# Two banks more for the first batch's scores, an earlier split of x, and weight decodes spread evenly in a fused attention and two-MLP kernel

## The chip, the cores and the metric

The kernel runs on one core of a Trainium2 chip. A core has a matrix engine (TensorE, PE in the profile, with its weight loads as PEld), VectorE (DVE), ScalarE (ACT), GpSimd (POOL) and SyncE (SP), which here issues every DMA. TensorE writes its results into PSUM banks, and the other engines read them there; everything else lies in SBUF. Each engine works through its own list of instructions in order and waits on semaphores for the others. The metric is the device time of one execution in microseconds (us), lower is better.

## The reference

The input is a batch of 4 with 8 heads, 576 positions and head size 64, all in 32-bit floats. Shortened to its arithmetic:

```
scores = scale * q @ k.T, causal mask;  local = softmax(scores) @ v
q_p = elu(q) + 1;  mem_out = (q_p @ M_prev) / (q_p . z_prev + 1e-6)
x = sigmoid(beta) * mem_out + (1 - sigmoid(beta)) * local     # to [2304, 512]
x = (s * relu(x @ w_in)**2 + b) @ w_out                       # first MLP, 2048 wide
h = x @ w2_in;  z = h * softmax(h)
out = (layernorm(z) * g_ln) @ w2_out                          # second MLP, 1024 wide
```

Weights and activations of the MLPs are split into a high and a low part, so that each of their products is three matmuls (high by high, low activation by high weight, high activation by low weight).

## The kernel before, in words

**Attention.** The heads are taken in pairs: 4 batches of 4 pairs, 16 pairs in all (`NPAIR` is 4, `u` counts the pairs). A pair goes through five steps of scores. `scores(u, 0, 1)`, then chunk 2, chunk 3 and the tail (`CF` is 4) each write one PSUM tile `s`, which `ps_s` gives out: it has a single buffer of two banks (L193, L305), one bank for each head of the pair, or for each half of the tail. VectorE reads the tile, adds the mask and finds the row's extreme (L331, L349), ScalarE takes the exponential (L298), TensorE transposes the result (L372), ScalarE copies the transposes out (L375), and `values` multiplies them with v (L404, L407) and adds the memory part (L409, L410). GpSimd multiplies v by the gate (L236), makes the product `q` for the memory's denominator (L251), and scales rows (L269, L270, L355). Transposes and values follow the scores with a lag of two steps.

**The weights.** They come as bit patterns that `decode` (L141 to L168) rebuilds: a DMA (L147), then one operation on ScalarE (L152), four on VectorE (L153, L154, L156, L158), one on GpSimd (L159), one more on ScalarE (L163) and one on VectorE (L164). 48 decodes serve the whole kernel. `decode_to(n)` asks for the first n of them, and where it is called sets how early a decode stands in the program.

**The first MLP** has two parts. `first_part` (five of the sixteen columns of weights, `FP1`) works on half batches of 288 tokens and serves as filler between the attention's steps: `split_x` makes `xh` on ScalarE (L442) and `xl` on VectorE (L443), `hidden` makes `h` (L424 to L426) with a relu on ScalarE (L427), a square on VectorE (L434) and the split parts `g` (L435, L438); then `y` (L471 to L473) is copied out by ScalarE (L475) and stored. During the attention `h` and `y` share `ps_m`, two buffers of one bank. What is left of the filler when the attention ends runs in a loop at L567 with PSUM tiles of its own for `h` (`ps_h`, two buffers). `second_part` does the other eleven columns in ten rounds of up to 512 tokens; a round loads `xr` from `xd` (L493), splits it with the same two lines (L442, L443) and runs `hidden` and `ystep` (L608 to L610). In round 0 the split is told to stand behind the last copy of the first part, `lastact` (L588). The second MLP follows.

**Order.** The kernel is built with a scheduler that takes the instructions as the code lists them and places them on each engine by its own estimate of when their operands are ready. So a buffer that is free earlier, or a decode that is called later, moves instructions on every engine. `issue_after` holds an instruction behind another one.

Of the kernel before, what the change touches and what calls it, by code (L numbers as in the profile page):

```python
# [8 lines left out]
F32 = mybir.dt.float32  # L9
# [3 lines left out]
AF = mybir.ActivationFunctionType  # L13
# [4 lines left out]
P = 128  # L18
# [5 lines left out]
def attention_mlp_kernel(  # L24
# [9 lines left out]
    nc = tc.nc  # L34
    B, NPAIR, _, NCH, _, D = q.shape
# [18 lines left out]
    big = const.tile([P, (CF + 1) * P], F32, name="big")  # L54
# [4 lines left out]
    HS = S // 2  # L59
    mtail = const.tile([P, HS], F32, name="mtail")  # L60
# [5 lines left out]
    gate = const.tile([P, H], F32, name="gate")  # L66
# [33 lines left out]
    RA = 2 * FP1 + 8  # L100
    RB = 25 - RA
# [68 lines left out]
    decoded = [0]  # L170
# [13 lines left out]
    QT = S + CF * P  # L184
# [3 lines left out]
    class Attention:  # L188
# [111 lines left out]
        def scores(self, u, *cs):  # L300


            p = self.pair[u]
            raw = p["raw"]
            ss = self.ps_s.tile([P, 2, 512], F32, tag="s", name=f"s{u}_{cs[0]}")  # L305
            if cs[0] == CF:
                self.tail_scores(u, ss)
                return
            c0 = 0
            at = {}  # L310
            for i in cs:
                for k in range(i + 1):
                    for j in range(2):
                        x = raw[j * D:(j + 1) * D]
                        self.last = nc.tensor.matmul(ss[:, j, c0 + k * P:c0 + (k + 1) * P],  # L315
                                                     x[:, S + i * P:S + (i + 1) * P], x[:, k * P:(k + 1) * P],
                                                     start=True, stop=True).ins
                at[i] = c0
                c0 += (i + 1) * P
            if "sums" not in p:  # L320
                p["sums"] = self.tiny.tile([P, NCH, 2], F32, tag="sums", name=f"sums{u}", bufs=2)

                nc.gpsimd.memset(p["sums"][:, CF], 1.0)
            for i in cs:
                n = (i + 1) * P
                prs, mxs = [], []
                for j in range(2):
                    pr = p["pr", 2 * i + j] = self.sp.tile([P, n], F32, tag=f"pr{i}", name=f"pr{u}_{i}_{j}")

                    mx = self.tiny.tile([P, 1], F32, tag="mx", name="mx")  # L330
                    nc.vector.tensor_tensor_reduce(pr, ss[:, j, at[i]:at[i] + n],  # L331
                                                   big[:, CF * P - i * P:CF * P - i * P + n],
                                                   -scale, FMAX, ALU.add, ALU.min, mx)
                    prs.append(pr)
                    mxs.append(mx)
                self.exps(prs, mxs, [p["sums"][:, i, e:e + 1] for e in (0, 1)])

        def tail_scores(self, u, ss):

            p = self.pair[u]  # L340
            raw = p["raw"]
            pr = p["pr", 2 * CF] = self.sp.tile([P, S], F32, tag="prt", name=f"pr{u}_t", bufs=1)
            mx = None
            for t in range(2):
                cols = slice(t * HS, (t + 1) * HS)
                nc.tensor.matmul(ss[:, t, 0:HS], raw[:, QT:RL], raw[:, cols], start=True, stop=True)
                m0 = FMAX if t == 0 else mx
                mx = self.tiny.tile([P, 1], F32, tag="mx", name="mx")
                nc.vector.tensor_tensor_reduce(pr[:, cols], ss[:, t, 0:HS], (big[:, cols], mtail)[t], -scale, m0,  # L349
                                               ALU.add, ALU.min, mx)  # L350
# [64 lines left out]


    attended = [False]
    lastact = [None]

    def hidden(w, xh, xl, n, ps, r, gh, gl, square=False):  # L420

# [25 lines left out]
    def first_part(b, pools):  # L447

        xs, gs, ys, _ = pools
        for sub in range(2):  # L450
            nm = f"{b}_{sub}"
            x = xbs[b][:, :, sub * N1:(sub + 1) * N1]
            xh = xs.tile([P, NC, N1], F32R, tag="xh", name=f"xh{nm}")
            xl = xs.tile([P, NC, N1], F32R, tag="xl", name=f"xl{nm}")
            split_x(x, xh, xl)
            gq = []
            for f in range(FP1):
                ps = pools[3][0].tile([P, 512], F32, tag="mh"[len(pools[3]) - 1], name=f"h{nm}_{f}")
                r = gs.tile([P, N1], F32, tag="r", name=f"r{nm}_{f}", bufs=2)
                g = gs.tile([P, 2, N1], F32R, tag="g", name=f"g{nm}_{f}")  # L460
                decode_to(f + 1)
                hidden(wtiles["in", f], xh, xl, N1, ps[:, 0:N1], r, g[:, 0], g[:, 1])
                gq.append(g)
                yield
            for c in range(NC):
                ps = pools[3][-1].tile([P, 512], F32, tag="m", name=f"y{nm}_{c}")
                o = ps[:, 0:N1]
                decode_to(2 * FP1)
                for f in range(FP1):
                    wc = [wtiles["out", f][:, t, c * P:(c + 1) * P] for t in range(2)]  # L470
                    nc.tensor.matmul(o, wc[0], gq[f][:, 0], start=(f == 0), stop=False)  # L471
                    nc.tensor.matmul(o, wc[1], gq[f][:, 0], start=False, stop=False)
                    nc.tensor.matmul(o, wc[0], gq[f][:, 1], start=False, stop=(f == FP1 - 1))  # L473
                y = ys.tile([P, N1], F32, tag="y", name=f"yo{nm}_{c}")
                lastact[0] = nc.scalar.activation(y, o, AF.Copy).ins  # L475
                t0 = b * S + sub * N1
                nc.sync.dma_start(yd[:, c, t0:t0 + N1], y)
                yield
# [19 lines left out]
    with ExitStack() as fctx:  # L498
# [65 lines left out]
        fpools[3] = [ps_h, ps_m]  # L564
        load2(0, False)
        attended[0] = True
        for it in filler:  # L567
            for _ in it:
                decode_to(min(decoded[0] + 1, RA + RB))

    def second_part():
        load2(0, True)
# [4 lines left out]
        for ri, (fs, bi) in enumerate(rounds):  # L577
# [10 lines left out]
            with tc.issue_after(lastact[0]) if ri == 0 else nullcontext():  # L588
                split_x(x[:, :, 0:n], xh[:, :, 0:n], xl[:, :, 0:n])
# [22 lines left out]
            for i, f in enumerate(fs):  # L612
                hstep(f)
                if i >= 1:
                    ystep(fs[i - 1])
                step += 1
                if ri == 0:
                    decode_to(min(decoded[0] + 2, g2))
                elif ri < len(blocks):

                    decode_to(g2 + (late - g2) * step // steps)
                elif ri < last:

                    decode_to(late + (last2 - late) * step // steps)
                else:
                    decode_to(decoded[0] + 1)
                if ri == last and i == 2:

                    z = dec.tile([P, WN, 2], I32, tag="raw", name="z0").rearrange("p n t -> p (n t)").bitcast(F32)
                    first["z"] = weights_of(0, z, *(const.tile([P, 1], F32, name=f"t0_{k}") for k in range(3)))  # L630
            if ri == last:
                decode_to(NW)
                first[1] = products(1)
# [164 lines left out]
```

## Time and profile before

| | us |
|---|---|
| median of 3 runs (lowest and highest) | 884.39 (883.9 to 886.73) |
| the profiled execution, device time | 885.48 |
| its span, first to last instruction | 883.70 |
| busy: PE, DVE, ACT, POOL | 850.8, 539.9, 513.7, 182.8 |

The profiled execution is 1.09 us above the median, and 1.78 us of it lie outside the span. TensorE is busy for 96% of the span, so what it does not do is 32.9 us in all. A busy TensorE is not one at its peak, since the ends of matmuls are modelled. The granted clock of TensorE is the full one, 2.4 GHz, except for one short stretch behind 375 us, where it is the lower level, 1.2 GHz.

### The profile page before, as it was taken

The page shows a single profiled execution, that of the slowest core. Times are in us where ns is not written, and L with a number is a line of the kernel's source. Part 1 is how long each engine was busy: PE and PEld are TensorE (multiplying, and loading weights), DVE is VectorE, ACT ScalarE, POOL GpSimd, SP SyncE. Part 2 cuts the span into 40 slices and gives each one's busy share as a digit, 9 for nine tenths or more (in the row PEclk, how much of TensorE's full clock was granted, in tenths as well). Part 3 has the DMA queues.
Part 4 walks back from the last instruction along what each step waited for, and adds up shares of the span by engine and source line. Part 5 has one row for each costly group of instructions (what it writes and reads, how often), then busy time and mean ns, then how long its engine had stood idle before and what let it go on. Part 6 is the DMA issues. An engine that isn't in the chain of part 4 may idle for free.

```text
span 883.7 us, 14245 instructions
## 1 busy us (share of the span) xinstructions
PE 850.8 (96%) x5344; PEld 699.0 (79%) x5344; DVE 539.9 (61%) x1236; ACT 513.7 (58%) x1094; POOL 182.8 (21%) x180
## 2 busy tenths in 40 slices
PE   7899889999999999899999999999999999999997
PEld 5677668888878878878888888888988888888885
DVE  3898986768778467922338864454775444454532
ACT  4776765666666665555558776556774333433332
POOL 4445351332333222200002311101120000000000
PEclk9999999999999999999999999999999999999999
DMA  7445242533343204472013422111200000000000
GB/s 228 133 148 184 79 155 59 155 97 119 115 149 118 69 1 156 147 263 95 3 45 114 144 100 96 48 48 55 89 24 1 25 25 23 13 24 24 25 25 36
DMA packets 41494, 76.44 MB, mean 86 GB/s; under 512 B 6352, under 2 KB 20176, under 8 KB 41424
## 3 DMA queue, kind: packets, MB, share of 16 engines
q1 hardware_dynamic: 41424, 75.52, 26.5%
q8 instruction: 42, 0.69, 0.3%
q14 instruction: 28, 0.23, 0.1%
HBM read 61.35 MB, written 14.16 MB: 85 GB/s over the span
## 4 chain that ended last, share of the span: by engine, by line
PE 78%; DVE 13%; ACT 3%; issue 2%; POOL 1%; DMA 1%; POOLq 0%; SPq 0%; ACTq 0%; DVEq 0%
PE h L424 7%; PE h L425 7%; PE h L426 7%; PE y L609 5%; PE y L608 5%; PE y L610 5%; PE h L665 4%; PE h L666 4%; PE h L667 4%; PE o L730 4%; PE o L729 4%; PE o L728 4%; PE pp L372 3%; PE s L315 3%; PE po L404 3%
## 5 line engine op out<-in xcount | busy, mean ns | idle before, releaser
L425 PE MATMUL h<-xl,w 128*128 128x512 f32 (+2 forms) x380 | 131.0, 345 | 2.1 <-DVE xl L443 2.1
L159 POOL TENSOR_TENSOR wa<-wa,raw 128x512 f32<-128x512 f32 x48 | 67.8, 1415 | 314.5 <-DVE raw L158 198.2
L424 PE MATMUL h<-xh,w 128*128 128x512 f32 (+2 forms) x380 | 130.0, 349 | 2.8 <-ACT xh L442 2.5
L426 PE MATMUL h<-xh,w 128*128 128x512 f32 (+2 forms) x380 | 129.2, 341 | 0.0
L427 ACT ACTIVATE r<-h 128x512 f32<-128x512 f32 (+2 forms) x95 | 45.6, 489 | 87.3 <-PE h L426 73.0
L298 ACT ACTIVATE pr<-pr,mx 128x128 f32<-128x128 f32 (+3 forms) x128 | 70.8, 555 | 37.5 <-DVE mx L331 37.5
L432 DVE TENSOR_TENSOR gl<-r,gh 128x512 fp32r<-128x512 f32 (+1 forms) x55 | 37.2, 685 | 88.1 <-ACT r L431 88.0
L424 PEld LDWEIGHTS h<-xh,w 128*128 128x128 f32 x380 | 70.9, 188 | 15.2 <-ACT xh L442 3.5
L425 PEld LDWEIGHTS h<-xl,w 128*128 128x128 f32 x380 | 71.5, 188 | 13.1 <-DVE xl L443 3.8
L608 PE MATMUL y<-gh,w 128*128 128x512 f32 (+1 forms) x220 | 80.8, 372 | 0.0
L609 PE MATMUL y<-gh,w 128*128 128x512 f32 (+1 forms) x220 | 80.8, 372 | 0.0
L426 PEld LDWEIGHTS h<-xh,w 128*128 128x128 f32 x380 | 71.5, 188 | 8.1 <-issue 0.4
L331 DVE CUSTOM_DVE_ANT_0 pr<-s,big 128x128 f32<-128x128 f32 (+3 forms) x128 | 56.2, 485 | 9.6 <-PE s L315 9.2
L375 ACT ACTIVATE pt<-pp 128x256 f32<-128x256 f32 (+2 forms) x96 | 47.2, 518 | 22.5 <-PE pp L372 22.0
L610 PE MATMUL y<-gl,w 128*128 128x512 f32 (+1 forms) x220 | 60.0, 372 | 0.0
L728 PE MATMUL o<-w,zh 128*128 128x512 f32 x144 | 56.8, 395 | 0.8 <-ACT zh L722 0.8
L730 PE MATMUL o<-w,zl 128*128 128x512 f32 x144 | 56.9, 395 | 0.6 <-DVE zl L723 0.6
L667 PE MATMUL h<-w,yl 128*128 128x512 f32 x144 | 56.6, 393 | 0.0
L729 PE MATMUL o<-w,zh 128*128 128x512 f32 x144 | 56.6, 393 | 0.0
L665 PE MATMUL h<-w,yh 128*128 128x512 f32 x144 | 56.6, 393 | 0.0
L666 PE MATMUL h<-w,yh 128*128 128x512 f32 x144 | 56.6, 393 | 0.0
L315 PEld LDWEIGHTS s<-kq 64*128 64x128 f32 x640 | 40.1, 187 | 19.3 <-issue 6.7
(142 smaller groups left out, 1959.1 us busy)
## 6 DMA issues: line engine op xcount, KB each, us to landing
raw<-in_moe_w_in_dram SPq DMA_DIRECT2D x24, 512.0 KB, 3.8
raw<-in_moe_w_out_dram SPq DMA_DIRECT2D x24, 512.0 KB, 3.5
kq<-in_kq_dram SPq DMA_DIRECT2D x16, 608.0 KB, 4.0
xr<-xd SPq DMA_DIRECT2D x8, 1024.0 KB, 5.9
q<-in_q_dram SPq DMA_DIRECT2D x16, 320.0 KB, 3.0
v<-in_v_dram SPq DMA_DIRECT2D x16, 320.0 KB, 3.1
xd<-xb SPq DMA_DIRECT2D x4, 1152.0 KB, 6.5
yd<-yo SPq DMA_DIRECT2D x32, 144.0 KB, 2.4
```

What stands on the lines that cost most here:

```text
L424: nc.tensor.matmul(ps, wc[0], xh[:, c, 0:n], start=(c == 0), stop=False)
L425: nc.tensor.matmul(ps, wc[0], xl[:, c, 0:n], start=False, stop=False)
L426: nc.tensor.matmul(ps, wc[1], xh[:, c, 0:n], start=False, stop=(c == NC - 1))
L608: nc.tensor.matmul(o, wc[0], gh[:, 0:n], start=(f == fs[0]), stop=False)
L609: nc.tensor.matmul(o, wc[1], gh[:, 0:n], start=False, stop=False)
L610: nc.tensor.matmul(o, wc[0], gl[:, 0:n], start=False, stop=(f == fs[-1]))
L665: nc.tensor.matmul(o, yh[:, c], w[:, 0], start=(c == 0), stop=False)
L666: nc.tensor.matmul(o, yh[:, c], w[:, 1], start=False, stop=False)
L667: nc.tensor.matmul(o, yl[:, c], w[:, 0], start=False, stop=(c == NC - 1))
L728: nc.tensor.matmul(oo, zh, w[:, 0], start=(f == 0), stop=False)
L729: nc.tensor.matmul(oo, zh, w[:, 1], start=False, stop=False)
L730: nc.tensor.matmul(oo, zl, w[:, 0], start=False, stop=(f == NF2 - 1))
```

## The change

Four edits. The scores of chunk 2 and of the tail, for the four pairs of the first batch, take two tiles of one bank from `ps_m` in place of the one tile of `ps_s`; so in this batch consecutive score tiles alternate between the two pools. The split of `xr` in round 0 is no longer held behind the last copy of the first part. The decodes are called at other places: in the filler's rest one in every fourth step in place of every step (5 in place of 7), in round 0 one in every second step in place of none beyond those already done (3), and from there evenly to the same count as before at the end of round 4. Three one-column constants of the second MLP's start lie in columns of the old `gate` tile.

```
--- before.py
+++ after.py
@@ -302,7 +302,12 @@
 
             p = self.pair[u]
             raw = p["raw"]
-            ss = self.ps_s.tile([P, 2, 512], F32, tag="s", name=f"s{u}_{cs[0]}")
+            if u < NPAIR and cs[0] in (2, CF):
+
+                ss = [ps_m.tile([P, 512], F32, tag="m", name=f"s{u}_{cs[0]}_{j}") for j in range(2)]
+            else:
+                ss = self.ps_s.tile([P, 2, 512], F32, tag="s", name=f"s{u}_{cs[0]}")
+                ss = [ss[:, j] for j in range(2)]
             if cs[0] == CF:
                 self.tail_scores(u, ss)
                 return
@@ -312,7 +317,7 @@
                 for k in range(i + 1):
                     for j in range(2):
                         x = raw[j * D:(j + 1) * D]
-                        self.last = nc.tensor.matmul(ss[:, j, c0 + k * P:c0 + (k + 1) * P],
+                        self.last = nc.tensor.matmul(ss[j][:, c0 + k * P:c0 + (k + 1) * P],
                                                      x[:, S + i * P:S + (i + 1) * P], x[:, k * P:(k + 1) * P],
                                                      start=True, stop=True).ins
                 at[i] = c0
@@ -328,7 +333,7 @@
                     pr = p["pr", 2 * i + j] = self.sp.tile([P, n], F32, tag=f"pr{i}", name=f"pr{u}_{i}_{j}")
 
                     mx = self.tiny.tile([P, 1], F32, tag="mx", name="mx")
-                    nc.vector.tensor_tensor_reduce(pr, ss[:, j, at[i]:at[i] + n],
+                    nc.vector.tensor_tensor_reduce(pr, ss[j][:, at[i]:at[i] + n],
                                                    big[:, CF * P - i * P:CF * P - i * P + n],
                                                    -scale, FMAX, ALU.add, ALU.min, mx)
                     prs.append(pr)
@@ -343,10 +348,10 @@
             mx = None
             for t in range(2):
                 cols = slice(t * HS, (t + 1) * HS)
-                nc.tensor.matmul(ss[:, t, 0:HS], raw[:, QT:RL], raw[:, cols], start=True, stop=True)
+                nc.tensor.matmul(ss[t][:, 0:HS], raw[:, QT:RL], raw[:, cols], start=True, stop=True)
                 m0 = FMAX if t == 0 else mx
                 mx = self.tiny.tile([P, 1], F32, tag="mx", name="mx")
-                nc.vector.tensor_tensor_reduce(pr[:, cols], ss[:, t, 0:HS], (big[:, cols], mtail)[t], -scale, m0,
+                nc.vector.tensor_tensor_reduce(pr[:, cols], ss[t][:, 0:HS], (big[:, cols], mtail)[t], -scale, m0,
                                                ALU.add, ALU.min, mx)
             sm = self.tiny.tile([P, 1], F32, tag="sm", name="sm")
             self.exps([pr], [mx], [sm])
@@ -415,7 +420,6 @@
 
 
     attended = [False]
-    lastact = [None]
 
     def hidden(w, xh, xl, n, ps, r, gh, gl, square=False):
 
@@ -472,7 +476,7 @@
                     nc.tensor.matmul(o, wc[1], gq[f][:, 0], start=False, stop=False)
                     nc.tensor.matmul(o, wc[0], gq[f][:, 1], start=False, stop=(f == FP1 - 1))
                 y = ys.tile([P, N1], F32, tag="y", name=f"yo{nm}_{c}")
-                lastact[0] = nc.scalar.activation(y, o, AF.Copy).ins
+                nc.scalar.activation(y, o, AF.Copy)
                 t0 = b * S + sub * N1
                 nc.sync.dma_start(yd[:, c, t0:t0 + N1], y)
                 yield
@@ -564,9 +568,11 @@
         fpools[3] = [ps_h, ps_m]
         load2(0, False)
         attended[0] = True
+        turn = 0
         for it in filler:
             for _ in it:
-                decode_to(min(decoded[0] + 1, RA + RB))
+                turn += 1
+                decode_to(min(decoded[0] + (turn % 4 == 0), RA + RB))
 
     def second_part():
         load2(0, True)
@@ -585,8 +591,7 @@
             x = xq.pop(ri)
             xh = xs2.tile([P, NC, NB], F32R, tag="xh", name=f"xh2_{ri}")
             xl = xs2.tile([P, NC, NB], F32R, tag="xl", name=f"xl2_{ri}")
-            with tc.issue_after(lastact[0]) if ri == 0 else nullcontext():
-                split_x(x[:, :, 0:n], xh[:, :, 0:n], xl[:, :, 0:n])
+            split_x(x[:, :, 0:n], xh[:, :, 0:n], xl[:, :, 0:n])
             ys = [ps_y.tile([P, 512], F32, tag=f"y{c}", name=f"y2_{ri}_{c}") for c in range(NC)]
             gq = {}
 
@@ -615,10 +620,11 @@
                     ystep(fs[i - 1])
                 step += 1
                 if ri == 0:
-                    decode_to(min(decoded[0] + 2, g2))
+                    decode_to(decoded[0] + step % 2)
+                    early = decoded[0]
                 elif ri < len(blocks):
 
-                    decode_to(g2 + (late - g2) * step // steps)
+                    decode_to(early + (late - early) * step // steps)
                 elif ri < last:
 
                     decode_to(late + (last2 - late) * step // steps)
@@ -627,7 +633,7 @@
                 if ri == last and i == 2:
 
                     z = dec.tile([P, WN, 2], I32, tag="raw", name="z0").rearrange("p n t -> p (n t)").bitcast(F32)
-                    first["z"] = weights_of(0, z, *(const.tile([P, 1], F32, name=f"t0_{k}") for k in range(3)))
+                    first["z"] = weights_of(0, z, *(gate[:, k:k + 1] for k in range(3)))
             if ri == last:
                 decode_to(NW)
                 first[1] = products(1)
```

How the first edit moves TensorE's list, from pair 0's tail scores on (`s_4` is the tail, `s_0`, `s_2`, `s_3` are the other steps; pair 0 reads `kq_139`, pair 1 `kq_165`; `pp` are transposes, `po` is values, `tr`, `tp`, `tq` are transposes for the memory part). Before:

```order
L346 MATMUL s_4_291<-kq_139 128x288
L404 MATMUL po_399<-pt_1_312,v_173 64x256 x6
L404 MATMUL po_399<-pt_1_312,v_173 64x128 x2
L315 MATMUL s_0_335<-kq_165 128x128 x6
L279 MATMUL tr_372<-ident,r_308 128x128 x4
L289 MATMUL tp_380<-ident,ph_175 128x128 x4
L292 MATMUL tq_386<-ident,ph_175 128x128
L315 MATMUL s_2_429<-kq_165 128x128 x6
L372 MATMUL pp_8_389<-ident,pr_t 128x128 x4
```

And now:

```order
L351 MATMUL s_4_0_292<-kq_139 128x288
L320 MATMUL s_0_337<-kq_165 128x128 x6
L351 MATMUL s_4_1_293<-kq_139 128x288
L377 MATMUL pp_6_362<-ident,pr_3_0_267 128x128 x4
L409 MATMUL po_401<-pt_0_253,v_173 64x256 x2
L409 MATMUL po_401<-pt_0_253,v_173 64x128
L377 MATMUL pp_7_368<-ident,pr_3_1_270 128x128 x4
L409 MATMUL po_401<-pt_0_253,v_173 64x128
L320 MATMUL s_2_0_431<-kq_165 128x128 x3
L320 MATMUL s_2_1_432<-kq_165 128x128 x3
L279 MATMUL tr_374<-ident,r_310 128x128 x4
```

Pair 1's first scores stand between the halves of pair 0's tail, and its second scores in front of the memory transposes. The first hidden products of the first MLP, which stood between the pairs of this batch, now stand behind the last of its scores.

GpSimd's list at the same place (`v_173` and `v_186` are the v of pairs 0 and 1, `q_167` is pair 0's product with z). Before:

```order
L232 TENSOR_TENSOR Mb_133<-Mb_133,gmt 128x512
L236 TENSOR_TENSOR v_173<-v_173,omg 128x640
L236 TENSOR_TENSOR v_186<-v_186,omg 128x640
L251 TENSOR_TENSOR q_167<-ph_175,zb_169 128x640
L270 TENSOR_TENSOR ph_175<-ph_175,den_180 128x640
```

And now:

```order
L232 TENSOR_TENSOR Mb_133<-Mb_133,gmt 128x512
L236 TENSOR_TENSOR v_173<-v_173,omg 128x640
L251 TENSOR_TENSOR q_167<-ph_175,zb_169 128x640
L236 TENSOR_TENSOR v_186<-v_186,omg 128x640
L270 TENSOR_TENSOR ph_175<-ph_175,den_180 128x640
```

Pair 0's product stands in front of pair 1's v.

ScalarE's list at the attention's end (`xb_3507` and `xb_3515` are the last batch's x, `raw` are weights to decode, `xr` is round 0's x). Before:

```order
L427 ACTIVATE r_1_4_4335<-h_1_4_4334 128x288
L442 ACTIVATE xh_0_4489<-xb_3507 128x288 x4
L435 ACTIVATE g_1_4_4336<-r_1_4_4335,b_sb 128x288
L152 ACTIVATE wa_4355<-raw_4353 128x512
L152 ACTIVATE wa_4386<-raw_4384 128x512
L152 ACTIVATE wa_4417<-raw_4415 128x512
L427 ACTIVATE r_0_0_4500<-h_0_0_4499 128x288
```

And now:

```order
L431 ACTIVATE r_1_4_4343<-h_1_4_4342 128x288
L446 ACTIVATE xh_0_4449<-xb_3515 128x288 x4
L439 ACTIVATE g_1_4_4344<-r_1_4_4343,b_sb 128x288
L152 ACTIVATE wa_4420<-raw_4418 128x512
L446 ACTIVATE xh_0_4878<-xr_4340 128x512 x4
L431 ACTIVATE r_0_0_4460<-h_0_0_4459 128x288
L431 ACTIVATE r_0_1_4479<-h_0_1_4478 128x288
```

The split of round 0 stood 44 rows behind the relu `r_0_0`, after the last copy `yo`; now it stands in front of that relu. On TensorE the first hidden products of round 0 stand between the last `y` of the first part.

## Rows read from the trace of the kernel before

**Rows 1.** Windows: stretch, length, busy us of each engine (instructions), clock, DMA.
```profile
14.00:74.00 60.00, 52.56 (x474) 39.15 (x475) 48.33 (x155) 43.01 (x114) 32.59 (x31) 1.00 0.51 157
74.00:130.00 56.00, 47.86 (x404) 35.39 (x404) 51.85 (x130) 39.89 (x103) 27.00 (x24) 1.00 0.42 131
130.00:335.00 205.00, 202.80 (x1738) 168.68 (x1735) 140.81 (x411) 134.05 (x352) 63.19 (x61) 1.00 0.32 99
335.00:400.00 65.00, 59.52 (x377) 52.64 (x376) 42.80 (x74) 35.16 (x76) 10.98 (x7) 0.97 0.63 206
```
**Rows 2.** Waits of TensorE, 14 to 74 us: total us, times, longest.
```profile
PE s L315 <- DVE mx L331: 2.2, 2, 1.5
PE po L404 <- POOL v L236: 1.7, 1, 1.7
PE s L346 <- DVE mx L349: 1.4, 1, 1.4
...
PE s L346 <- DVE mx L331: 0.2, 1, 0.2
```
**Rows 3.** Timeline of GpSimd and VectorE, 15 to 19 us: start, length, instruction, wait.
```profile
15.38 1.25 POOL L236 TENSOR_TENSOR v<-v,omg 128x640 f32<-128x640 f32 x1 [0.45 <-DMA v<-in_v_dram]
16.59 1.55 POOL L251 TENSOR_TENSOR q<-ph,zb 128x640 f32<-128x640 f32 x1
...
18.18 0.82 DVE L254 TENSOR_REDUCE den<-q 128x10 f32<-128x640 f32 x1 [4.59 <-POOL q L251]
```
**Rows 4.** Line L154 over the whole span: min, median, max ns.
```profile
L154 DVE SCALAR_TENSOR_TENSOR wa<-raw,wa x48: 676/690/1808, 22.9 to 652.4; 128x512 int32<-128x512 int32 x48
```
**Rows 5.** Waits of TensorE, 338 to 392 us.
```profile
PE h L424 <- ACT xh L442: 1.9, 2, 1.1
PE h L425 <- DVE xl L443: 1.4, 1, 1.4
PE y L471 <- ACT g L435: 1.1, 1, 1.1
PE y L473 <- DVE g L438: 0.4, 1, 0.4
PE y L471 <- ACT yo L475: 0.3, 1, 0.3
```
**Rows 6.** Windows of TensorE's fall of the clock.
```profile
374.00:376.00 2.00, 0.62 (x3) 0.30 (x2) 2.00 (x5) 1.40 (x4) 0.15 (x1) 1.00 0.74 221
376.00:378.00 2.00, 1.88 (x8) 1.88 (x9) 1.39 (x3) 0.50 (x2) 0.00 (x0) 0.56 0.52 199
378.00:380.00 2.00, 1.74 (x9) 1.39 (x8) 0.00 (x0) 0.71 (x2) 0.00 (x0) 0.58 0.00 0
380.00:382.00 2.00, 2.00 (x17) 2.00 (x17) 0.00 (x0) 0.04 (x1) 0.00 (x0) 1.00 0.43 148
```
**Rows 7.** Timeline of ScalarE, around the attention's end, and round 0's split.
```profile
341.11 1.80 ACT L152 ACTIVATE wa<-raw 128x512 f32<-128x512 f32 x3
343.92 0.71 ACT L427 ACTIVATE r<-h 128x288 f32<-128x288 f32 x2 [1.02 <-PE h L426]
...
384.25 2.18 ACT L442 ACTIVATE xh<-xr 128x512 fp32r<-128x512 f32 x4
```
**Rows 8.** Load of round 0's x: issue on SP, its landing; landing of the next load.
```profile
337.51 0.57 SPq L493 DMA_DIRECT2D xr<-xd  x1
...
DMA to landing us min/median/max: 6.9/6.9/6.9
...
DMA to landing us min/median/max: 11.4/11.4/11.4
```
**Rows 9.** Windows: VectorE in the filler's rest.
```profile
340.00:360.00 20.00, 18.54 (x132) 17.65 (x133) 19.84 (x39) 13.10 (x31) 4.68 (x3) 1.00 0.67 215
```
**Rows 10.** Waits of TensorE, 400 to 850 us.
```profile
PE h L425 <- DVE xl L443: 0.7, 1, 0.7
```

More of the change, by code (lines that the diff above doesn't have):

```diff
@@ L304, in scores @@
             raw = p["raw"]
-            ss = self.ps_s.tile([P, 2, 512], F32, tag="s", name=f"s{u}_{cs[0]}")
+            if u < NPAIR and cs[0] in (2, CF):
+                ss = [ps_m.tile([P, 512], F32, tag="m", name=f"s{u}_{cs[0]}_{j}") for j in range(2)]
+            else:
+                ss = self.ps_s.tile([P, 2, 512], F32, tag="s", name=f"s{u}_{cs[0]}")
+                ss = [ss[:, j] for j in range(2)]
             if cs[0] == CF:
@@ L314, in scores @@
                         x = raw[j * D:(j + 1) * D]
-                        self.last = nc.tensor.matmul(ss[:, j, c0 + k * P:c0 + (k + 1) * P],
+                        self.last = nc.tensor.matmul(ss[j][:, c0 + k * P:c0 + (k + 1) * P],
                                                      x[:, S + i * P:S + (i + 1) * P], x[:, k * P:(k + 1) * P],
@@ L330, in scores @@
                     mx = self.tiny.tile([P, 1], F32, tag="mx", name="mx")
-                    nc.vector.tensor_tensor_reduce(pr, ss[:, j, at[i]:at[i] + n],
+                    nc.vector.tensor_tensor_reduce(pr, ss[j][:, at[i]:at[i] + n],
                                                    big[:, CF * P - i * P:CF * P - i * P + n],
@@ L345, in tail_scores @@
                 cols = slice(t * HS, (t + 1) * HS)
-                nc.tensor.matmul(ss[:, t, 0:HS], raw[:, QT:RL], raw[:, cols], start=True, stop=True)
+                nc.tensor.matmul(ss[t][:, 0:HS], raw[:, QT:RL], raw[:, cols], start=True, stop=True)
                 m0 = FMAX if t == 0 else mx
                 mx = self.tiny.tile([P, 1], F32, tag="mx", name="mx")
-                nc.vector.tensor_tensor_reduce(pr[:, cols], ss[:, t, 0:HS], (big[:, cols], mtail)[t], -scale, m0,
+                nc.vector.tensor_tensor_reduce(pr[:, cols], ss[t][:, 0:HS], (big[:, cols], mtail)[t], -scale, m0,
                                                ALU.add, ALU.min, mx)
@@ L417, in attention_mlp_kernel @@
     attended = [False]
-    lastact = [None]
     def hidden(w, xh, xl, n, ps, r, gh, gl, square=False):
@@ L474, in first_part @@
                 y = ys.tile([P, N1], F32, tag="y", name=f"yo{nm}_{c}")
-                lastact[0] = nc.scalar.activation(y, o, AF.Copy).ins
+                nc.scalar.activation(y, o, AF.Copy)
                 t0 = b * S + sub * N1
@@ L566, in attention_mlp_kernel @@
         attended[0] = True
+        turn = 0
         for it in filler:
             for _ in it:
-                decode_to(min(decoded[0] + 1, RA + RB))
+                turn += 1
+                decode_to(min(decoded[0] + (turn % 4 == 0), RA + RB))
     def second_part():
@@ L587, in second_part @@
             xl = xs2.tile([P, NC, NB], F32R, tag="xl", name=f"xl2_{ri}")
-            with tc.issue_after(lastact[0]) if ri == 0 else nullcontext():
-                split_x(x[:, :, 0:n], xh[:, :, 0:n], xl[:, :, 0:n])
+            split_x(x[:, :, 0:n], xh[:, :, 0:n], xl[:, :, 0:n])
             ys = [ps_y.tile([P, 512], F32, tag=f"y{c}", name=f"y2_{ri}_{c}") for c in range(NC)]
@@ L617, in second_part @@
                 if ri == 0:
-                    decode_to(min(decoded[0] + 2, g2))
+                    decode_to(decoded[0] + step % 2)
+                    early = decoded[0]
                 elif ri < len(blocks):
-                    decode_to(g2 + (late - g2) * step // steps)
+                    decode_to(early + (late - early) * step // steps)
                 elif ri < last:
@@ L629, in second_part @@
                     z = dec.tile([P, WN, 2], I32, tag="raw", name="z0").rearrange("p n t -> p (n t)").bitcast(F32)
-                    first["z"] = weights_of(0, z, *(const.tile([P, 1], F32, name=f"t0_{k}") for k in range(3)))
+                    first["z"] = weights_of(0, z, *(gate[:, k:k + 1] for k in range(3)))
             if ri == last:
```

## The prediction

> **What bounds the kernel now.** I read the windows by stage first. TensorE is busy for 202.8 of 205 us between 130 and 335 us [rows 1], and between 400 and 850 us its only wait is one of 0.7 us [rows 10]. In both stretches the time is TensorE's work, and this change removes none of it. Time can only come from the places where TensorE stands idle: 7.4 us between 14 and 74 us, 8.1 us between 74 and 130, 5.5 us between 335 and 400 (length less busy time, [rows 1]). The reader is to see what else is full there. Between 14 and 74 us VectorE is busy for 48.3 of 60 us; between 74 and 130 for 51.9 of 56: TensorE and VectorE wait for each other. Next I read who ends TensorE's waits in these stretches [rows 2, 5], then the lists of the changed kernel at these places.
>
> **The scores of the first batch.** In the first stretch the waits for the one score tile to come free are 2.2, 1.4 and 0.2 us, 3.8 us together [rows 2]; a score matmul stands there until VectorE has read the tile before. With the second pair of banks the tile before that one is enough, and TensorE's new list puts pair 1's first scores between the halves of pair 0's tail. So these 3.8 us should go. The 1.7 us for v stay, since the same v stands in GpSimd's list at the same place. What could be next: VectorE, which still has to read each tile. In the stretch it has 11.7 us to spare. About 1.7 us of this goes as well: GpSimd made pair 0's product q at 16.59 us, behind pair 1's v and its wait of 0.45 us; now q is in front, and VectorE's sum of it, which began at 18.18 us, can begin some 1.7 us sooner (0.45 and 1.25, [rows 3]). The hidden products that were in this stretch move behind pair 3's scores. That costs nothing as long as TensorE's 8.1 idle us of the next stretch hide them; without this cover it is an exchange of places, since TensorE does them once in either case. From both sides: at best all 7.4 idle us of this stretch go; at worst nothing does, because pairs 4 to 7 keep the one score tile and VectorE is 93% busy there. I take 3.8 us, the waits that have a name.
>
> The trace has the 48 L154 operations at 0.68 us at least, 0.69 in the middle and 1.81 at most [rows 4]: some of them are stretched. The Trainium skill, SBUF — State Buffer, section Who interferes with whom, states that a VectorE instruction with two SBUF inputs and a GpSimd instruction that reads SBUF take turns, and the second waits until the first is done. L154 has two SBUF inputs, so by that page a tighter first batch, with VectorE and GpSimd both fuller, would have more such turns; the trace agrees in so far as its longest exceeds its shortest by 1.1 us. By that rule the sum would lose its 3.8 us, as in rival (a), and come out at 882.0. I do not forecast it, since the middle one of the 48 is an undisturbed one.
>
> **The split of round 0's x.** What goes: round 0's first matmul waits 1.1 us for its split (the longer of two waits that make 1.9), and in the last quarter of the filler TensorE waits 1.4, 1.1, 0.4 and 0.3 us for VectorE and ScalarE [rows 5]. Round 0's hidden products, which the early split allows between the last y, fill these; and the stretch has two decodes fewer on VectorE, which was busy for 19.8 of 20 us [rows 9]. Sum 4.3 us. The other 0.8 us of the 1.9 stays, its operations stand as before. A clock effect comes on top. Behind the stretch of 374 to 376 us, in which TensorE was busy for 0.62 of 2 us, the granted clock reads 0.56 and 0.58, the lower level for part of it; 17 matmuls took 3.62 us of busy time where the next 17 took 2.00 [rows 6]. So the fall costs 1.6 us. Up to 5.9 us can go.
>
> What comes: the early split has to wait for its load. The load is issued when the attention has ended, at 337.51 us, and lands 6.9 us later, at 344.4 [rows 8]. ScalarE now has one decode in front of the split where it had three, so it arrives at 341.11 plus a third of 1.80, at 341.7 us, and stands for 2.7 us; the split itself takes 2.18 us [rows 7], to 346.6. The relu behind it, which ran at 343.92, is 2.7 us late. The hidden product after that needs the relu's PSUM tile, since there are two, and TensorE has nothing else in front of it: about 2.6 us of a new wait. The copies of y and the next relu are queued behind the split too, but they are needed later than that product. VectorE's part of the split (four operations) waits with it, and SP's queue has the next x load in front of the weight loads; both have time, as the decodes are fewer. I leave 0.4 us of the removed waits in place, since VectorE's work now starts later. Whether the clock falls behind the new wait is open: the row before the old fall had 1.4 idle us in 2, with smaller pauses around it, and the new wait is longer. I charge half of 1.6. Sum: 5.9 less 2.6, 0.4 and 0.8 is 2.1 us saved. Bounds: 5.9 (the load is early or something else fills the wait) and a loss of 2.8 (below).
>
> **The decodes and the constants.** Between 400 and 850 us there is 0.7 us of waiting in all [rows 10]; spread decodes can save at most that, and I take 0.3. A decode that comes too late would cost, but round 0 to round 4 still end with the same count. The constants' new place changes no instruction: nothing, hidden by the fact that no row reads or writes more; a wait on an old reader of the tile is the only cost, and that reader ran at the start. Changed order between 130 and 335 us can move the 2.2 idle us there by as much either way; I take zero.
>
> **The sum.** 3.8 + 2.1 + 0.3 = 6.2 us from the profiled execution's 885.48 us gives 879.3. The median of the runs is 1.1 us lower than that execution, so 878.2 us is the forecast; the rivals below are on the same footing (884.4 less their savings).
>
> **Rivals.** (a) VectorE is the bound. What the first batch wins is given back before 130 us, where VectorE has 4.1 idle us of 56 [rows 1]. The same comes out if one operation like L154 is stretched once more in each of the four pairs, by the 1.1 us between its shortest and its longest [rows 4]: 4.4 us, more than the 3.8. For it: these rows, and score waits of pairs 4 to 7 that no edit touches. Against it: the change also fills VectorE's idle time by the 1.7 us of q. Only 2.4 us are left: 882.0 us.
> (b) More than forecast. All 7.4 idle us of the first stretch go, the clock does not fall, nothing of the old waits remains (5.9 less 2.6 is 3.3), and 0.7 in the rounds: 11.4 us, 873.0 us. For it: TensorE loses the hidden products in that stretch and VectorE starts sooner. Against it: v's wait stays.
> (c) The load is as late as the next one, which took 11.4 us [rows 8]. Then the new wait is 4.5 us longer, 7.1, and the clock falls with all of 1.6: the edit loses 7.1 + 1.6 less 5.9, 2.8 us. With 3.8 and 0.3 saved elsewhere this is 883.1 us. Against it: that later load ran beside others, and the first one's neighbour is the same as before.
> (d) Slower: scores that stand further ahead block TensorE's list. TensorE takes its matmuls in the order of the list; a score that waits for VectorE holds the transposes and values behind it, so ScalarE's copies and the next pair's work start late. If decodes on VectorE come in between and two scores of each of the four pairs wait as long as the longest of now, 1.5 us [rows 2], the waits are 12 us in place of 3.8, a loss of 8.2; with 2.4 saved elsewhere the time is 890.2 us. It decides from 6.2 us of score waits in the first batch on, which is 3.8 and the 2.4. Against it: the tile that must be free is one further back.
> That the change does not do what it says can be excluded: the lists show all three moves.
>
> **How the numbers follow.** Forecast 0.50, its own range 875 to 881.5; (a) 0.18, of which the stretching 0.05; (b) 0.15; (c) 0.07; (d) 0.10. A measurement of this kernel can tell about 0.3%, 2.7 us, from no change: faster means below 881.7, slower above 887.1. Nearly all of the forecast, all of (b) and a third of (a) are faster, 0.69; (c) and the rest of (a) are within, with a little of the forecast, 0.19; (d) and what spills over from (c) is slower, 0.12. The range from 873 to 886 leaves out (d) and half of (b).
>
> **What would show it.** Right: score waits in the first batch near zero, pair 0's sum of q near 16.5 us, an attention that ends about 4 us before 337; then ScalarE standing in front of the split for some 2.7 us after the last xb split, a TensorE wait of about 2.6 us on that relu, and no waits over 0.5 us on g or round 0's split after it. Wrong: score waits that move to pairs 4 to 7, an attention's end within 1 us of now, or a wait at the split beyond 5 us. The prediction as a whole falls if the time is above 882 us.

## The result, and the profile after

The changed kernel takes 871.44 us (median of 4 runs, 870.01 to 873.01) against 884.89 us for the kernel before (4 runs, 883.90 to 886.73): a ratio of 0.9846, with a 95% interval from 0.9817 to 0.9875. It is 13.5 us faster, where 6.2 were forecast, and 1.6 us below the low end of the stated range (873 to 886). The profiled execution has a span of 868.2 us against 883.7.

First the windows by stage of the kernel after, with the columns of [rows 1].

```profile
14.00:74.00 60.00, 55.14 (x473) 40.42 (x473) 55.92 (x159) 43.29 (x117) 32.49 (x31) 1.00 0.50 156
74.00:130.00 56.00, 51.97 (x435) 40.28 (x433) 48.02 (x126) 39.76 (x101) 28.07 (x24) 0.97 0.45 143
130.00:335.00 205.00, 202.88 (x1743) 167.97 (x1742) 142.02 (x414) 133.91 (x352) 62.19 (x60) 1.00 0.31 95
335.00:400.00 65.00, 61.84 (x379) 57.00 (x378) 41.81 (x73) 37.20 (x77) 9.94 (x7) 0.97 0.59 194
```

TensorE's idle time (length less busy) is now 4.9, 4.0 and 3.2 us in the three stretches where it was 7.4, 8.1 and 5.5. VectorE is at 55.9 of 60 us in the first, where it was at 48.3, with 159 operations for 155: it has little more to do there and takes longer over it. The largest rise is that of L153, an operation of the decodes; its lines for this stretch, before and then after, end in the count, the busy us, the mean ns, and the idle time in front:

```profile
L153 DVE TENSOR_SCALAR wa<-wa 128x512 int32<-128x512 int32 x5 | 2.3, 455 | 0.2 <-ACT wa L152 0.2
L153 DVE TENSOR_SCALAR wa<-wa 128x512 int32<-128x512 int32 x6 | 5.2, 866 | 0.2 <-ACT wa L152 0.2
```

The 0.97 in the second stretch is a fall of TensorE's clock to the lower level, 3.4 us long, that the kernel before did not have there:

```profile
106.00:108.00 2.00, 0.58 (x2) 0.12 (x2) 2.00 (x4) 0.37 (x1) 2.00 (x2) 0.98 0.49 134
108.00:110.00 2.00, 1.95 (x14) 1.73 (x15) 1.97 (x6) 1.97 (x4) 0.55 (x3) 0.50 0.46 178
```

TensorE's waits between 14 and 74 us of the kernel after answer to [rows 2].

```profile
PE tr L279 <- POOL r L269: 2.4, 3, 1.3
PE s L320 <- DVE mx L354: 1.3, 2, 0.7
PE pe L412 <- ACT ptl L384: 0.6, 1, 0.6
PE pe L412 <- DVE ptl L387: 0.4, 1, 0.4
```

The score waits fell from 3.8 to 1.3 us, and the wait of 1.7 us on v is gone. The waits of the memory transposes on GpSimd grew from 0.6 us, a line of the kernel before that [rows 2] leave out:

```profile
PE tr L279 <- POOL r L269: 0.6, 1, 0.6
```

The timeline of GpSimd and VectorE answers to [rows 3].

```profile
14.54 1.55 POOL L251 TENSOR_TENSOR q<-ph,zb 128x640 f32<-128x640 f32 x1
16.04 1.26 POOL L236 TENSOR_TENSOR v<-v,omg 128x640 f32<-128x640 f32 x1
16.12 0.82 DVE L254 TENSOR_REDUCE den<-q 128x10 f32<-128x640 f32 x1 [2.87 <-POOL q L251]
```

The sum of q begins at 16.12 us, where about 16.5 was forecast. The attention ends at 333.95 us, 3.4 us earlier. Next the timeline of ScalarE at round 0's split, for [rows 7].

```profile
337.70 0.66 ACT L152 ACTIVATE wa<-raw 128x512 f32<-128x512 f32 x1
340.74 2.19 ACT L446 ACTIVATE xh<-xr 128x512 fp32r<-128x512 f32 x4 [2.38 <-DMA xr<-xd]
342.84 0.68 ACT L431 ACTIVATE r<-h 128x288 f32<-128x288 f32 x2
```

ScalarE stands for 2.4 us in front of the split, as forecast (2.7), and the relu is late. TensorE's waits from 336 us to the end answer to [rows 5, 10].

```profile
PE h L428 <- ACT r L431: 2.3, 1, 2.3
PE o L734 <- ACT zh L728: 0.9, 1, 0.9
PE h L428 <- ACT xh L446: 0.8, 1, 0.8
PE o L736 <- DVE zl L729: 0.6, 1, 0.6
PE h L429 <- DVE xl L447: 0.3, 1, 0.3
```

The waits on xl, g and yo at the end of the first part are gone; one of 2.3 us on the relu came (2.6 forecast). The clock fell again, now behind this wait, as the windows of TensorE show, which answer to [rows 6].

```profile
342.00:344.00 2.00, 0.72 (x3) 0.72 (x4) 2.00 (x5) 2.00 (x6) 0.00 (x0) 0.86 0.30 115
344.00:346.00 2.00, 2.00 (x10) 2.00 (x10) 2.00 (x5) 0.66 (x2) 0.00 (x0) 0.50 0.43 148
346.00:348.00 2.00, 2.00 (x14) 2.00 (x14) 1.46 (x3) 0.43 (x2) 1.51 (x1) 0.78 0.83 196
```

So far nearly everything is as forecast, and yet half of the gain isn't there. What lies behind the attention's end took 546.3 us before (883.7 less 337.4) and takes 534.2 now, 12.1 less; my terms for it gave 2.4. Much of it comes in the rounds and the second MLP, where TensorE's only wait between 400 and 850 us was one of 0.7 us [rows 10]: VectorE's first sum of the second part into yT (L638, now L644) began at 418.9 us and now begins at 410.1 (8.8 earlier), the last products with yh in the second MLP's first layer (L665, now L671) begin 15.2 us earlier (858.2 and 843.0). TensorE reads as busy there in both kernels; now its matmuls are closer together.

### The profile page after: what moved, and what is told of

Its sections match the earlier page's. It is cut to its first block, busy times and chain, and to the rows that moved or that the text cites. A ratio compares the mean times of both kernels' runs of the same rounds, so it can differ in the third digit from the quotient of the medians.

```text
span 868.2 us, 14223 instructions
## 1 busy us (share of the span) xinstructions
PE 846.5 (97%) x5344; PEld 703.6 (81%) x5344; DVE 539.8 (62%) x1236; ACT 513.0 (59%) x1094; POOL 180.4 (21%) x180
## 4 chain that ended last, share of the span: by engine, by line
PE 80%; DVE 12%; ACT 2%; DMA 2%; POOL 2%; issue 2%; SPq 0%; POOLq 0%; ACTq 0%; DVEq 0%
PE h L428 7%; PE h L430 7%; PE h L429 7%; PE y L614 5%; PE y L613 5%; PE y L615 5%; PE h L673 4%; PE h L672 4%; PE h L671 4%; PE o L736 4%; PE o L734 4%; PE o L735 4%; PE po L409 3%; PE pp L377 3%; PE s L320 3%; PE y L475 2%
## 5 line engine op out<-in xcount | busy, mean ns | idle before, releaser
L428 PEld LDWEIGHTS h<-xh,w 128*128 128x128 f32 x380 | 72.0, 190 | 12.9 <-ACT r L431 3.0
L430 PEld LDWEIGHTS h<-xh,w 128*128 128x128 f32 x380 | 72.3, 190 | 7.7 <-issue 0.6
L320 PE MATMUL s<-kq 64*128 64x128 f32 x640 | 55.1, 292 | 3.1 <-DVE mx L354 2.7
L320 PEld LDWEIGHTS s<-kq 64*128 64x128 f32 x640 | 44.5, 191 | 15.7 <-issue 7.1
L734 PE MATMUL o<-w,zh 128*128 128x512 f32 x144 | 56.3, 391 | 0.9 <-ACT zh L728 0.9
L671 PE MATMUL h<-w,yh 128*128 128x512 f32 x144 | 56.5, 392 | 0.0
```

What stands on the lines that cost most here:

```text
L320: self.last = nc.tensor.matmul(ss[j][:, c0 + k * P:c0 + (k + 1) * P], x[:, S + i * P:S + (i + 1) * P], x[:, k * P:(k + 1) * P], start=True ...
L428: nc.tensor.matmul(ps, wc[0], xh[:, c, 0:n], start=(c == 0), stop=False)
L430: nc.tensor.matmul(ps, wc[1], xh[:, c, 0:n], start=False, stop=(c == NC - 1))
L671: nc.tensor.matmul(o, yh[:, c], w[:, 0], start=(c == 0), stop=False)
L734: nc.tensor.matmul(oo, zh, w[:, 0], start=(f == 0), stop=False)
```

## The experiments

**Where the rounds' time went.** I went through all records of 512-column matmuls behind the attention and took the time from one start to the next. In the kernel after it is 227 ns for nearly every one; in the kernel before some were at 227 and others at 234, without any wait. What tells them apart is where the tiles lie in SBUF, which the built program lists. A matmul reads its moving operand from there, and the weights of the next are loaded meanwhile: in the first window below, weight loads (the second number) are busy for 48 of 60 us in which no matmul waits. The three one-column constants each took 32 bytes of every partition ahead of the weights' pool; in the gate tile they take none, and the weights lie 96 bytes lower. Four kernels were run on that. These are the edits of the first two, e1 and e2; e3 has 16 columns in place of 8, and e4 undoes the first edit in the kernel after.

```diff
-first["z"] = weights_of(0, z, *(const.tile([P, 1], F32, name=f"t0_{k}") for k in range(3)))
+first["z"] = weights_of(0, z, *(gate[:, k:k + 1] for k in range(3)))
```
```diff
 warm = const.tile([P, 256], mybir.dt.bfloat16, name="warm")
+pad = const.tile([P, 8], F32, name="pad")
```

> The kernel before with the third edit alone: the three constants of the second MLP's start lie in columns of the old gate tile. Theory (addresses): three tiles of 32 bytes less move every tile behind them, the weights among them, by 96 bytes; then no 512-column matmul reads its moving operand and the weights of the next from different halves of 64 bytes, where 996 pairs behind the attention did, and those were 7.0 ns slower in the trace of before (233.9 against 227 ns from start to start). 996 x 7.0 ns = 7.0 us, with the 256-column ones up to 8: 877.4 us. Rival (the moved split and the spread decodes gave the whole difference, constants cost nothing as I had predicted): 884.9 us within 1.

Measured: 877.42 us against 884.63, ratio 0.9918 (0.9898 to 0.9937). The constants alone are worth 7.2 us (5.6 to 9.0 by the interval).

> The kernel before with one unused tile of 32 bytes among the constants; every engine's instructions and their order are those of before, only addresses move by 32 bytes. Theory (halves of 64 bytes): as e1, 877.4 us, matmuls of 512 columns 227 ns apart throughout. Rival (it is the use of the gate's columns or the freed space, not the address): 884.9 us. Rival (nothing but the other edits count): 884.9 us.

Measured: 883.69 us, ratio 0.9993 (0.9981 to 1.0005). My theory of halves of 64 bytes fell: all pairs lie in the same half, and 988 of them still take 232.6 ns.

> The kernel before with one unused tile of 64 bytes among the constants; instructions and order as before, addresses move by 64 bytes. Theory (what counts is whether the two operands lie in the same half of 64 bytes): as before, 884.9 us within 1, and the slow pairs are the same ones, 234 ns. Rival (any other address, or a distance of other size, helps): near 877 us.

Measured: 884.31 us, ratio 0.9997 (0.9987 to 1.0008); the same pairs at 233.6 ns. Expected, but it tells little after e2.

> The changed kernel with the three constants back in tiles of their own; the scores, the split and the decodes stay changed. Theory (addresses): loses what e1 wins, 871.4 + 7.5 = 878.9 us, which is about the forecast of 878.2 us, since the forecast held the other three edits. Rival (split and decodes gave everything): 871.4 us.

Measured: 877.05 us, ratio 0.9914 (0.9900 to 0.9928). The other three edits together give 7.6 us, the constants on top of them the rest, from 0.9914 to 0.9846, about 6 us.

Two more pads of the kernel before, `[P, 104]` and `[P, 40]`, ask for the right period:

> The kernel before with one unused tile of 416 bytes among the constants; instructions and order as before. The half of 64 bytes fell with the 32-byte tile: there all pairs lay in the same half, and 988 of them were still 232.6 ns from start to start. In the traces so far a 512-column matmul takes 227 to 229 ns where its moving operand and the weights of the next have the same address modulo 256 and 512, and 232.6 to 233.9 where they differ by 96, 128 or 160 bytes. With 416 bytes more the weights lie at 480 modulo 512, as the operands of the second part do. Theory (same place within 256 or 512 bytes): all pairs at 227 ns, 884.6 - 7.2 = 877.4 us, as with the constants moved. Rival (it isn't the address but the constants in gate, or the space): 884.6 us.

Measured: 877.51 us against 883.84, ratio 0.9927 (0.9912 to 0.9942).

> The kernel before with one unused tile of 160 bytes; instructions and order as before. Weights at 224 modulo 512, the operands of the second part at 480: the same place modulo 256, not modulo 512. Theory 256: all pairs 227 ns, 877.4 us. Theory 512: 988 pairs at 232 to 234 ns, 884.6 us.

Measured: 877.12 us, ratio 0.9924 (0.9909 to 0.9940). An unused tile of 160 bytes, with every instruction and its order unchanged, makes the kernel before 6.7 us faster, so it is the address, and the place counts modulo 256, not 512. The table is worked out from the records of the 512-column matmuls behind the attention: number, and mean time from start to start, of those whose moving operand and next weights have the same address modulo 256, and of the others. Starts 300 ns or more apart, where TensorE waited or ran at the lower clock, are left out.

```
kernel               18 weight tiles   same place       other place
before                      64        901, 227.8 ns    988, 233.9 ns
32 bytes more (e2)          96        901, 228.0       988, 232.6
64 bytes more (e3)         128        901, 228.5       988, 233.6
160 bytes more (e6)        224       1889, 227.1         0
416 bytes more (e5)        224       1882, 227.1         0
constants alone (e1)       224       1890, 227.1         0
after, old constants (e4)   64        902, 227.7       992, 233.9
after                      224       1895, 227.1         0
```

The operands of the second part and the other seven weight tiles are at 224 in all of them; the yh and zh of the second MLP move with the 18. The same can be seen in one view of the profile if one reads the count beside the busy time. A window in the rounds, of the kernel with 64 bytes more, and then of the one with 160:

```profile
400.00:460.00 60.00, 60.00 (x259) 48.42 (x258) 19.17 (x31) 33.69 (x52) 1.31 (x1) 1.00 0.09 28
```

```profile
400.00:460.00 60.00, 60.00 (x266) 49.67 (x266) 19.39 (x31) 33.81 (x53) 1.30 (x1) 1.00 0.10 33
```

Busy for 60.00 of 60 us at the full clock in both, and 259 matmuls against 266: 2.7% more in the same time.

**The scores alone.** The edit is the first one of the diff, put into the kernel before.

> The kernel before with the first edit alone (scores of chunk 2 and of the tail in the first MLP's banks for the first four pairs). My term was 3.8 us: 884.6 - 3.8 = 880.8 us, the attention ending near 333.7 us. Rival (a) of the prediction, given back before 130 us: above 882 us. Rival (b): all of 7.4 us, 877.2 us.

Measured: 881.65 us against 883.84, ratio 0.9969 (0.9957 to 0.9981), by the ratio 2.7 us (1.7 to 3.8). The mechanism is right, the size at the edge. The attention's end in a single profile says little: without this edit it came between 334.9 us (e1) and 337.7 us (e5). But the profiles of all kernels tell the two groups apart: nine without the edit have a mean of 336.6 us, five with it 333.4 to 334.5 and a mean of 333.9, 2.7 us earlier.

**The split and the decodes**, together and each alone, in the kernel before. The edits:

```diff
-            with tc.issue_after(lastact[0]) if ri == 0 else nullcontext():
-                split_x(x[:, :, 0:n], xh[:, :, 0:n], xl[:, :, 0:n])
+            split_x(x[:, :, 0:n], xh[:, :, 0:n], xl[:, :, 0:n])
```
```diff
+        turn = 0
...
-                decode_to(min(decoded[0] + 1, RA + RB))
+                turn += 1
+                decode_to(min(decoded[0] + (turn % 4 == 0), RA + RB))
...
-                    decode_to(min(decoded[0] + 2, g2))
+                    decode_to(decoded[0] + step % 2)
+                    early = decoded[0]
...
-                    decode_to(g2 + (late - g2) * step // steps)
+                    decode_to(early + (late - early) * step // steps)
```

> The kernel before with the second and the fourth of the diff's places, the split of round 0's x unordered and the decodes spread; scores and constants as before. My terms were 2.1 and 0.3 us: 884.6 - 2.4 = 882.2 us. From the changed kernel with the old constants (877.1 us) less the scores' 3.8 it should be 880.9 us, 3.7 us saved, if the parts add up. Rival (split loses by a late load): 887 us.

Measured: 878.28 us against 883.84, ratio 0.9931 (0.9915 to 0.9947), by the ratio 6.1 us.

> The kernel before with the unordered split of round 0's x alone; decodes, scores and constants as before. Split and spread decodes together saved 0.69% of the time (6.1 us), where my terms gave 2.4. Theory (the split carries it, its decodes on VectorE only help): 4 us or more of the 6.1, so 880 us or less. Rival (the seven decodes of the filler's rest stand in front of the split and of the y copies, so the early split without fewer decodes wins little): 883 us, ScalarE reaching the split after its load has landed and TensorE still waiting over 1 us on g.

Measured: 881.17 us against 884.67, ratio 0.9953 (0.9937 to 0.9969), 4.2 us by the ratio (2.7 to 5.6). The time is near the theory's, the waits on g are near the rival's. Its waits of TensorE from 334 us on:

```profile
PE h L424 <- ACT r L427: 2.7, 1, 2.7
PE y L473 <- DVE g L438: 0.9, 2, 0.6
PE h L424 <- ACT xh L442: 0.8, 1, 0.8
...
PE h L425 <- DVE xl L443: 0.7, 1, 0.7
```

> The kernel before with the spread decodes alone; the split still held behind the last copy of the first part. Theory (the split carries it): 883.5 us, 0.5 to 1 saved, TensorE still idle for over 2 us at the end of the first part. Rival (the decodes on VectorE, 19.8 of 20 us busy there, were the cause of the waits): 880 us, the waits on xl, g and yo gone.

Measured: 878.71 us, ratio 0.9929 (0.9914 to 0.9944), by the ratio 6.3 us (5.0 to 7.6): as much as both together. Its waits from 334 us on:

```profile
PE h L424 <- ACT xh L442: 1.9, 2, 1.1
PE o L731 <- ACT zh L725: 0.8, 1, 0.8
PE o L733 <- DVE zl L726: 0.6, 1, 0.6
PE y L471 <- ACT yo L475: 0.4, 1, 0.4
```

And VectorE and TensorE in the filler's rest, where [rows 9] has 19.84 and 18.54 us:

```profile
340.00:360.00 20.00, 19.94 (x147) 19.51 (x148) 16.89 (x33) 10.96 (x27) 2.82 (x2) 1.00 0.56 188
```

So the rival of e10 was right: the decodes on VectorE made the waits on xl and g, and with five of them in this stretch, one in every fourth step, in place of seven these are gone; the one on yo (0.4 us) stayed. The early split takes the waits on round 0's x (1.9 us) down to 0.8, and brings one of 2.3 to 2.7.

**The split behind its load.** In the kernel after:

```diff
-        nc.scalar.activation(r, ps, AF.Relu)
+        lastact[0] = nc.scalar.activation(r, ps, AF.Relu).ins
...
+                if turn == 8:
+                    held[0] = lastact[0]
...
+            with tc.issue_after(held[0]) if ri == 0 else nullcontext():
...
```

> The changed kernel with round 0's split held behind the relu of the third hidden product of the first part's last half: its load has landed by then, so ScalarE doesn't stand in front of it. Theory: the new wait of TensorE (2.3 us in the changed kernel) goes, and the fall of the clock behind it (13 matmuls at 240 ns in place of 133, 1.4 us): 871.4 - 3.7 = 867.7 us. Rival (what is behind the split on ScalarE and VectorE is now later, and round 0's first products wait for it): 871.4 us.

Measured: 867.11 us, ratio to the kernel before 0.9802 (0.9782 to 0.9821), and to the kernel after, by the two ratios, 0.9955 (about 0.992 to 0.999). ScalarE no longer waits for the load:

```profile
339.97 0.71 ACT L433 ACTIVATE r<-h 128x288 f32<-128x288 f32 x2 [2.14 <-PE h L432]
...
343.45 2.18 ACT L448 ACTIVATE xh<-xr 128x512 fp32r<-128x512 f32 x4
```

TensorE's waits from 331 us to the end:

```profile
PE o L739 <- ACT zh L733: 0.9, 1, 0.9
PE h L430 <- ACT xh L448: 0.8, 1, 0.8
PE o L741 <- DVE zl L734: 0.6, 1, 0.6
PE pp L377 <- ACT R L281: 0.3, 1, 0.3
PE h L431 <- DVE xl L449: 0.3, 1, 0.3
```

The wait on the relu is gone, and so is the clock's fall behind it. It is the fastest of all kernels here, 4.3 us better than the changed one by the medians and 3.9 by the ratios, where 3.7 were expected.

**The identity's place.** Two unused tiles, in the kernel after:

```diff
+    pad0 = const.tile([P, 88], F32, name="pad0")
     ident = const.tile([P, P], F32, name="ident")
...
+    pad1 = const.tile([P, 40], F32, name="pad1")
```

> The changed kernel with two unused tiles, of 352 bytes in front of the identity matrix and of 160 bytes behind the constants: the identity, which is the moving operand of all 624 transposes, comes to the same place modulo 256 as their stationary tiles (it was 128 against 224), all other operands keep theirs; instructions and order unchanged. Theory (the place matters for 128 columns as for 512): a quarter of 7 ns for each, 624 x 1.7 ns = 1.1 us, 870.3 us, transposes at 107 ns from start to start in place of 109. Rival (short matmuls have time to spare): 871.4 us, 109 ns.

Measured: 872.10 us, ratio to the kernel before 0.9854 (0.9836 to 0.9873), the kernel after's within its interval; the transposes stay 109 ns apart. The 128-column transposes gain nothing. Nor do the 256-column matmuls of the rounds: those with weights at another place are 117.7 ns from start to start in the profile of before (same place: 119.3), and with all at the same place, in e6, they are 119.7.

## Why the prediction was wrong

**The step that failed: "The constants' new place changes no instruction: nothing, hidden by the fact that no row reads or writes more."** The first half is true, and e6 shows the second to be no reason: with no instruction changed at all, a move of the weights is worth 6.7 us. In the kernel before, 988 matmuls were 7 ns slower than need be: 988 × (233.9 - 227.1) is 6.7 us, and the constants alone gave 7.2 (e1). My windows had shown TensorE busy throughout the rounds, and I concluded that time could only come from where it stands idle [rows 1, 10]. It was busy and slow, and the start-to-start times would have shown two kinds of the same matmul.

**The other three edits** were forecast at 6.2 us and gave 7.6 (e4: 877.05 us, forecast 878.2). That is close, but with other shares, and so in part luck.

- Scores, 3.8 us: the mechanism holds, the size does not quite. Score waits fell to 1.3 us, the sum of q starts at 16.12 us, and the score waits between 74 and 130 us, those of pairs 4 to 7 among them, fell from 4.3 to 2.1 us. The edit alone gives 2.7 us (1.7 to 3.8). Two waits beside it were misjudged: the 1.7 us for v, said to stay, went, with pair 1's first scores now in front of these values in TensorE's list; and the wait on GpSimd's r, for which I had no term, went from 0.6 to 2.4 us.
- Rival (d) did not come about. Of rival (a) the stretching did: between 14 and 130 us VectorE's operations take 22.9 us more in sum than if each took as long as the shortest of its line and shape in the run, where it was 19.3 before (22.2 to 23.3 in the five kernels with this edit, 17.8 to 19.3 in the nine without). That is 3.6 us more, of 4.4 in (a), but e7 shows that the gain is not given back. L153 is among them, which reads one tensor only; so two inputs, as the prediction had it, are not what all of it needs. What stretches them is not shown.
- Split, 2.1 us, and decodes, 0.3 us: 6.1 together, mis-sized and put down to the wrong edit. The 4.3 us of waits that go were booked on round 0's products filling the gaps; e10 shows that the decodes remove most of these waits by themselves, for 6.3 us. I had the row for it, VectorE at 19.8 of 20 us [rows 9], and used it only as an aside. The new wait was sized well: 2.6 forecast, 2.3 in the kernel after, 2.7 in e8 and e9. The sum went by idle time, which understates these waits, since the record of a 288-column matmul is some 290 ns long and the next starts 133 ns after it. From the attention's end to round 0's last product TensorE is idle for 5.5 us in the profile of before; counted by the starts that come over 60 ns late, 9.0 us are lost, and 1.2 more to the clock. By that count it is 4.7 us in e10, 6.8 in e9, 4.7 and 1.5 for the clock in e8, and 2.0 in e11. That places 5.6 us of e10's 6.3 and 4.1 of e8's 6.1; the rest stays open.
- The clock fall of 1.6 us [rows 6] was no sure gain. With the kernel before's list at that place, the profiles of e1, e3, e5 and e7 show no fall between 370 and 385 us, those of e2 and e6 one of 6.8 us. One execution's fall is not a property of the list. In the kernel after there is one behind the new wait: 13 matmuls at 240 ns from start to start in place of 133, 1.4 us; e11 has neither wait nor fall there. The other fall of the kernel after, at 107.9 us, stands behind 2 us in which TensorE was busy for 0.58, and was in no term: ten 128-column matmuls are 213 to 214 ns apart in it, in place of 109 to 112, about 1 us by estimate. All five profiles with the changed scores have one such fall between 20 and 124 us, at four different places, and three of the nine others have one. Whether the edit brings it on is not shown.

Rival (b), more than forecast, had the right side and the wrong reason: it counted the idle time alone, 11.4 us, and could go no further. The sum of the single edits (2.7, 6.1 and 7.2) is 16.0; together they give 13.5 (11.1 to 16.2 by the interval), so that they may overlap a little. Which waits they share was not tried.

## What to carry to other kernels

A busy engine is no bound until its pace has been looked at: count the instructions of one shape per window, or take the time from start to start, and ask why some are slower than the fastest. The same count shows what a wait costs where the idle time shows only a part of it. An edit that allocates or frees a tile moves every tile behind it; where long chains of 512-column matmuls run without a pause, compare the operands' addresses modulo 256, and try an unused tile as a pad, which costs one line. Where an early step must wait for a load, hold it behind work that is there anyway: of an engine's list, the place behind the landing is worth more than the earliest one.

## What the runs showed of the hardware

After a 512-column matmul of this kernel the next starts 227.1 to 228.5 ns later where its moving operand and the weights loaded beside it have the same address modulo 256, and 232.6 to 233.9 ns later where they differ by 96, 128 or 160 bytes. It is the pair that counts: in the kernel before, weights at 64 were fast as the moving operand of the second MLP's yh at 64 (227.4 ns), and slow beside xh, gh and gl at 224 (234 ns). Whether the next weights count or those in use isn't settled: only 63 matmuls of that profile tell the two apart, and they lie between (229.9 and 231.4 ns). Differences of 32 and 64 bytes weren't tried. For 128-column transposes e12 shows no effect, and the 256-column matmuls show none. The Trainium skill, TensorE: Matmul & The Clock Gate, section Step-by-step: what each phase is for, says that loading the next weights takes no SBUF read bandwidth from the running matmul, as each has its own read port. By that the places of the two could not matter, and the time would be the 884 us of e3 in e6 as well; the measured 877.12 us differs, and it decides. Why the places matter stays open: no run here looks inside.
